# A windowed attention with a two-layer feed-forward: three of chunk 0's four head pairs in another arithmetic form, and three moves at the start

## The chip, the cores and the metric

The kernel runs on one core of a Trainium2 chip. The metric is the device time of one execution in microseconds. Before the change, three runs gave a median of 1069.58 us (1069.06 to 1069.76). One more execution was taken with the profiler; its own time is in the table below.

The names of the engines in the profile: PE is the matrix engine (TensorE) and PEld its weight load, DVE is VectorE, ACT is ScalarE, POOL is GpSimd, SP is the queue that issues most transfers. A name with a small q behind it (ACTq, SPq) is that engine's instruction queue, where transfers are issued.

## What is computed

```python
# q, k, v: 8 batches x 8 heads x 576 positions x 64
scores = scale * np.matmul(q, k.transpose(0, 1, 3, 2))
mask = (rel >= 0) & (rel < 128)              # a window of 128 positions
scores = np.where(mask, scores + bias, -1e9) # bias: slope of the head times distance
attn = softmax(scores)
x = (attn @ v), heads side by side           # 4608 tokens x 512
h = x @ w_in                                 # 512 x 2048
g = np.where(h >= 1, h, np.where(h <= -1, 0, (h + 1) ** 2 / 4))
out = g @ w_out                              # 2048 x 512
```

The weights w_in and w_out are given in double precision (64 bits), so the kernel has to convert them itself; everything else is float32.

## The kernel before, in words

The 4608 tokens are cut into 12 chunks of 384 (three blocks of 128). A chunk has eight heads, taken as four pairs, so there are 48 pairs `p` and 96 heads `m`: pairs 0 to 3 with heads 0 to 7 belong to chunk 0, pairs 4 to 7 to chunk 1, and so on. Each chunk then goes through the feed-forward in 16 steps `fc`, each with a slice of 128 of the 2048 hidden columns: `layer1` (12 products into one PSUM bank, L363 to L365), the activation (L372 on ScalarE, L373 and L374 on VectorE), and `layer2` (into three accumulator banks, L393 or L396 to L398).

One head goes through these steps:

- `scores` (L220): products of q and k into PSUM (L243 or L245, L246); VectorE adds the bias and mask and finds the row's extreme (L249, tile `z`); ScalarE takes the exponential and its sum (L251); VectorE takes the reciprocal of the sum (L257, L258) and folds the two halves of the window, scaled, into `ep` (L262, L264). There is one buffer `z`, so the next head's L249 can start only when this head's fold is done.
- `weights_t` (L267): three transposes on PE (L273), a copy out of PSUM on ScalarE (L276 or L283, tile `lu`), and two selects on GpSimd (L277 and L279, or L286 and L288) that cut the window's triangles.
- `values` (L292): products of these with v into `x`, then a copy into `xn`, which the feed-forward's `split_x` (L350) cuts into a high part `xh` (L356, ScalarE) and a low part `xl` (L357, VectorE).

There are two forms. In the **plain** form the products take float32 operands with 64 rows (q times k, L243) or 64 columns (L314). In the **split** form each operand is cut into a high part in the type fp32r and the rest; the two parts lie side by side in the 128 rows or columns of the array, and there are two products for each block (L245 and L246; L338). The split form costs more operations outside PE: `prepare_q` takes two ScalarE and two VectorE operations (L198, L199) for one ScalarE operation (L193); `prepare_k` (L208 ScalarE, L209 VectorE) and `prepare_v` (L217, L218) exist only there; `weights_t` has one more VectorE operation (L284) and selects twice as wide; `values` ends with one copy and two additions for each head (L339, L340, L342). In chunk 0 before, a pair's two heads write into the two halves of one bank, and one copy (L319) takes both out.

`LIGHT = 2` makes the first two chunks plain. The loads of k are into tag `kr`, and for odd pairs of the plain form into tag `kk`, which is otherwise the split form's high part; each tag has one buffer. The same holds for v with tags `vn` and `vs`.

The order of the work: `segments` is a list of all attention steps, head by head, up to head 13 in the order scores, preparation of the next pair, `weights_t` of the head before, `values` of the head before that. During chunk 0's attention the weights of the first feed-forward steps are fetched (L123 and L129, on ScalarE's queue) and converted (`convert_in` and `convert_out`, L113 to L116, L135 and L136), at the places that `EARLY` lists. After `values(7)` the feed-forward's steps follow, with the attention of the next chunk spread between them. The framework's scheduler then orders the instructions of each engine by readiness, with the program's order as priority; on the chip each engine runs them strictly in that order. `behind(ins, f)` adds an ordering on the engine of `ins`: what `f` issues on that engine comes after `ins`.

Of the kernel before, what the change touches and what calls it, by code (L numbers as in the profile page):

```python
# [8 lines left out]
F32 = mybir.dt.float32  # L9
# [9 lines left out]
def windowed_attention_then_ffn(  # L19
# [37 lines left out]
    assert 2 * SEQ == CYCLE * CH and CYCLE == 3 and CUT == P + D  # L57
    NEG = -1.0e30

    LIGHT = 2  # L60

# [16 lines left out]
    quarter = const.tile([P, 1], F32, name="quarter")  # L78
    G.memset(quarter, 0.25)
    qscale = const.tile([P, NPAIR], F32, name="qscale")  # L80
    for g in range(NPAIR):
# [71 lines left out]
    head = {}  # L153
    xn = {}
    done_t = {}
    lo_rows = [slice(0, D), slice(D, P)]
# [6 lines left out]
    def load_qk(p):  # L163

        c, g = divmod(p, NPAIR)
        n = CH + before(c) * P
        st = pair[p] = {}
        qr = st["qr"] = ap1.tile([P, CH], F32, name=f"qr_{p}", tag="qr")
        DMA.dma_start(qr, q[g * P:(g + 1) * P, c * CH:(c + 1) * CH])
        kr = st["kr"] = ap1.tile([P, 2, CH + P], F32, name=f"kr_{p}", tag="kk" if c < LIGHT and p % 2 else "kr")  # L170
        if c < LIGHT:
            DMA.dma_start(kr[:, 0, :n], k[g * P:(g + 1) * P, (c + 1) * CH - n:(c + 1) * CH])
            return
        for half in (slice(0, D), slice(D, P)):
            DMA.dma_start(kr[half, :, :n],
                          k[g * P:(g + 1) * P, (c + 1) * CH - n:(c + 1) * CH].rearrange("(j d) t -> d j t", j=2))

    def load_v(p):
        c, g = divmod(p, NPAIR)
        nb = NQB + before(c)  # L180
        if c < LIGHT and p % 2:
            t = ap1.tile([P, 2, NQB + 1, 2, D], F32, name=f"vn_{p}", tag="vs")[:, 0]
        else:
            t = ap1.tile([P, NQB + 1, 2, D], F32, name=f"vn_{p}", tag="vn")
        pair[p]["vn"] = t
        DMA.dma_start(t[:, :nb].rearrange("p i j d -> p i (j d)"),
                      v[(c + 1) * CH - nb * P:(c + 1) * CH, g * P:(g + 1) * P].rearrange("(i p) d -> p i d", p=P))

    def prepare_q(p):
        ql = pair[p]["ql"] = ap1.tile([P, 2, CH], F32R, name=f"ql_{p}", tag="ql")  # L190
        qr = pair[p]["qr"]
        if p // NPAIR < LIGHT:
            S.activation(ql[:, 0].bitcast(F32), qr, AF.Copy, scale=qscale[:, p % NPAIR:p % NPAIR + 1])  # L193
            return
        for j in range(2):
            scale = 2.0 ** (2 * (p % NPAIR) + j + 1) / 8.0
            o_hi, o_lo, s = ql[lo_rows[j], j], ql[hi_rows[j], j], qr[lo_rows[j]]
            S.mul(o_hi, s, scale)  # L198
            V.scalar_tensor_tensor(o_lo, s, scale, o_hi.bitcast(F32), ALU.mult, ALU.subtract)  # L199

    def prepare_k(p):
        if p // NPAIR < LIGHT:
            return
# [7 lines left out]
    def prepare_v(p):  # L211
        if p // NPAIR < LIGHT:
            return
# [6 lines left out]
    def scores(m, blks):  # L220
# [14 lines left out]
        for n, i in enumerate(blks):  # L235
# [4 lines left out]
            win.append((o, c0, lone))  # L240
            if c < LIGHT:
                r, qs, ks = lo_rows[j], slice(i * P, (i + 1) * P), slice(k0, k0 + 2 * P - c0)
                T.matmul(o, ql[r, 0, qs].bitcast(F32), kr[r, 0, ks], start=True, stop=True)  # L243
                continue
# [22 lines left out]
    def weights_t(m):  # L267
# [4 lines left out]
        for i in range(NQB):  # L272
            T.transpose(pt[:, i, :], ep[:, i, :], ident)  # L273
        if m < LIGHT * H:
            own = lu[:, 0, 1::2, :].bitcast(F32)
# [16 lines left out]
    def values(m):  # L292
# [4 lines left out]
        if j == 0:  # L297
            xn[c, g] = xp1.tile([P, CH], F32, name=f"xn_{c}_{g}", tag=f"xn{g}")
        if c == 0:

            if j == 0:
                pair[p]["px"] = ps_acc.tile([P, DM], F32, name=f"x_{m}", tag="acc")
            pb = pair[p]["px"]
        else:
            pb = bank(f"x_{m}")
        px, pf = pb[:, :CH], pb.rearrange("r (i w) -> r i w", w=P)
        o = xn[c, g][lo_rows[j]]
        if c < LIGHT:
            po = px[lo_rows[j]] if c == 0 else px[:D]
            todo = [i for i in (0, 1, 2, -1) if i + b0 >= 0]  # L310
            for n, i in enumerate(todo):
# [4 lines left out]
                         start=(n == 0), stop=(n == len(todo) - 1), skip_group_check=True)  # L316
            if c == 0:
                if j:
                    (V.tensor_copy if g % 2 else S.copy)(xn[c, g], px)  # L319
            elif j:  # L320
                S.copy(o, po)
# [8 lines left out]
        for n, (i, s) in enumerate(todo):  # L330
# [5 lines left out]
            else:  # L336
                ox, lx = px[:, q0 * P:q1 * P], lu[:, s, first:first + q1 - q0, :].rearrange("p a w -> p (a w)")
            T.matmul(ox, w, lx, start=(n == 0), stop=(n == len(todo) - 1), skip_group_check=True)  # L338
        S.copy(o, px[D:, :])  # L339
# [98 lines left out]
    for i in range(NCHUNK * NFC + LAG):  # L438
        c, fc = divmod(i, NFC)
        ops = []  # L440
        if c < NCHUNK:
            if fc == 0:
                ops.append(lambda c=c: split_x(c))
            ops.append(lambda c=c, fc=fc: layer1(c, fc))
            if c == 0:
# [28 lines left out]
    load_v(0)  # L474
    prepare_q(0)
    prepare_k(0)
    load_qk(1)
    for fc in range(2):
        fetch_weights(fc)
    for t, m in enumerate(EARLY):  # L480
# [45 lines left out]
```

## Time and profile before

| | |
|---|---|
| median of three runs | 1069.58 us |
| the profiled execution, its own time | 1071.97 us |
| its span (first to last instruction) | 1070.3 us |
| mean granted TensorE clock over the span | 0.99 |
| PE busy | 1034.4 us (97%) |
| VectorE busy | 790.2 us (74%) |
| ScalarE busy | 619.1 us (58%) |
| GpSimd busy | 370.6 us (35%) |

The page gives busy times of whole executions. Other views used below: the windows give the busy time of each engine in chosen stretches of the span, with the granted TensorE clock; the chain of waits follows the work that ended last back in time; the timeline lists instructions with their start and duration; the groups by line give the count, the total and the mean duration (ns) of one kind of instruction, behind the second bar its idle time in front; the issues of transfers give KB and the time from issue to landing. Within brackets a row of the timeline tells how long the engine stood idle before it and what released it.

### The profile page before, as it was taken

Reading aid. Unit: us, or ns where it says so; the run is one execution under the profiler, and the core shown is the slowest. Engines: PE = TensorE matmul, PEld = TensorE weight load, DVE = VectorE, ACT = ScalarE, POOL = GpSimd, SP = SyncE. Lnnn points to the kernel's source line nnn. Section 1 sums busy time; section 2 is a strip of 40 time slices with the busy share of each in tenths; the row PEclk is TensorE's granted clock in tenths of the full one; section 3 lists DMA queues with packets and bytes.
Section 4 is the critical chain, followed back from the end, with each engine's and each line's share of the span. In section 5 each row is a group of like instructions: output and inputs, shape, how many; then the busy total and the mean of one; then the engine's idle time right before and its main releaser. Section 6 shows DMA issues by size and latency. Waiting matters only on the chain.

```text
span 1070.3 us, 16779 instructions
## 1 busy us (share of the span) xinstructions
PE 1034.4 (97%) x5472; PEld 900.9 (84%) x5472; DVE 790.2 (74%) x2249; ACT 619.1 (58%) x1475; POOL 370.6 (35%) x419
## 2 busy tenths in 40 slices
PE   6899999999999999999999999999999999999998
PEld 3566667998988988998998989899899889899996
DVE  3687799888887688877678887767787897862322
ACT  4686876556655556556557556555565665742322
POOL 2121003334443343443343443443334444332221
PEclk9889999999999999999999999999999999999999
DMA  5455512121122122121211212111121221200000
GB/s 190 139 188 189 175 45 69 34 59 60 45 65 67 39 62 79 33 56 35 66 47 50 82 47 65 63 30 37 60 65 37 77 65 38 76 1 1 30 1 30
DMA packets 58903, 69.50 MB, mean 65 GB/s; under 512 B 4032, under 2 KB 44480, under 8 KB 58816
## 3 DMA queue, kind: packets, MB, share of 16 engines
q1 hardware_dynamic: 48064, 51.66, 16.8%
q10 hardware_dynamic: 10752, 16.78, 4.5%
q8 instruction: 43, 0.70, 0.3%
q14 instruction: 44, 0.36, 0.1%
HBM read 58.98 MB, written 9.44 MB: 64 GB/s over the span
## 4 chain that ended last, share of the span: by engine, by line
PE 82%; DVE 8%; ACT 5%; issue 2%; POOL 2%; DMA 0%; ACTq 0%; DVEq 0%; POOLq 0%
PE h L363 11%; PE h L364 11%; PE h L365 11%; PE acc L396 10%; PE acc L397 10%; PE acc L398 10%; PE x L338 5%; PE acc L393 3%; PE p L273 3%; PE s L246 2%; PE s L245 2%; PE x L314 2%; PE s L243 2%; ACT z L251 1%; POOL lu L288 1%
## 5 line engine op out<-in xcount | busy, mean ns | idle before, releaser
L382 POOL TENSOR_TENSOR gl<-g,gh 128x384 fp32r<-128x384 f32 x176 | 184.1, 1046 | 434.9 <-ACT gh L381 422.0
L363 PE MATMUL h<-xh,wi 128*128 128x384 f32 x768 | 265.0, 345 | 1.8 <-ACT sg L372 1.6
L364 PE MATMUL h<-xl,wi 128*128 128x384 f32 x768 | 260.3, 339 | 0.6 <-DVE xl L357 0.6
L365 PE MATMUL h<-xh,wi 128*128 128x384 f32 x768 | 259.4, 338 | 0.0
L396 PE MATMUL acc<-wo,gh 128*128 128x512 f32 x528 | 211.8, 401 | 8.1 <-ACT gh L381 8.1
L373 DVE SCALAR_TENSOR_TENSOR g<-sg 128x384 f32<-128x384 f32 x192 | 108.6, 565 | 150.4 <-ACT sg L372 139.0
L397 PE MATMUL acc<-wo,gh 128*128 128x512 f32 x528 | 207.8, 394 | 0.0
L381 ACT CAST gh<-g 128x384 fp32r<-128x384 f32 x176 | 90.4, 513 | 192.5 <-DVE g L374 182.1
L372 ACT ACTIVATE sg<-h,quarter 128x384 f32<-128x384 f32 x192 | 111.2, 579 | 141.4 <-PE h L365 140.6
L251 ACT ACTIVATE z<-z,nmax 128x256 f32<-128x256 f32 (+2 forms) x288 | 139.2, 486 | 33.8 <-DVE nmax L249 31.7
L398 PE MATMUL acc<-wo,gl 128*128 128x512 f32 x528 | 155.5, 398 | 0.0
L363 PEld LDWEIGHTS h<-xh,wi 128*128 128x128 f32 x768 | 144.5, 188 | 11.0 <-ACT sg L372 3.2
L364 PEld LDWEIGHTS h<-xl,wi 128*128 128x128 f32 x768 | 144.5, 188 | 7.2 <-issue 2.0
L365 PEld LDWEIGHTS h<-xh,wi 128*128 128x128 f32 x768 | 144.4, 188 | 0.0
L249 DVE CUSTOM_DVE_ANT_0 z<-s,rel 128x256 f32<-128x256 f32 (+2 forms) x256 | 94.3, 394 | 52.8 <-PE s L246 43.3
L264 DVE CUSTOM_DVE_ANT_0 ep<-z,rc 128x128 f32<-128x128 f32 x256 | 129.4, 546 | 1.5
L286 POOL TENSOR_SCALAR_AFFINE_SELECT lu<-lu 128x768 fp32r<-128x768 f32 x80 | 80.7, 1008 | 128.7 <-DVE lu L284 120.1
L396 PEld LDWEIGHTS acc<-wo,gh 128*128 128x128 f32 x528 | 99.4, 188 | 27.3 <-ACT gh L381 10.5
L374 DVE SCALAR_TENSOR_TENSOR g<-sg,g 128x384 f32<-128x384 f32 x192 | 111.9, 583 | 3.7
L398 PEld LDWEIGHTS acc<-wo,gl 128*128 128x128 f32 x528 | 97.0, 188 | 19.7 <-POOL gl L382 0.2
L397 PEld LDWEIGHTS acc<-wo,gh 128*128 128x128 f32 x528 | 99.4, 188 | 16.5
L288 POOL TENSOR_SCALAR_AFFINE_SELECT lu<-lu 128x768 fp32r<-128x768 f32 x80 | 81.3, 1017 | 4.6
(78 smaller groups left out, 1451.4 us busy)
## 6 DMA issues: line engine op xcount, KB each, us to landing
kr<-in_k_dram SPq DMA_DIRECT2D x60, 256.0 KB, 3.8
qr<-in_q_dram SPq DMA_DIRECT2D x48, 192.0 KB, 3.4
out_dram<-o SPq DMA_DIRECT2D x36, 256.0 KB, 2.3
rawi<-in_moe_w_in_dram ACTq DMA_DIRECT2D x16, 512.0 KB, 3.9
rawo<-in_moe_w_out_dram ACTq DMA_DIRECT2D x16, 512.0 KB, 5.0
vn<-in_v_dram SPq DMA_DIRECT2D x32, 256.0 KB, 2.7
kr<-in_k_dram SPq DMA_DIRECT2D x28, 192.0 KB, 3.2
vn<-in_v_dram SPq DMA_DIRECT2D x16, 192.0 KB, 2.5
```

The costliest lines, as they stand in the source:

```text
L251: S.activation(z[:, i, c0:], z[:, i, c0:], AF.Exp, bias=nmax[:, i:i + 1], scale=-1.0, accum_out=sm[:, i, 0:1])
L264: st["folded"] = V.tensor_tensor_reduce(out=ep[:, i, :], in0=z[:, i, :P], in1=z[:, i, P:], op0=ALU.add, op1=ALU.add, scale=rc[:, i:i + 1], ...
L363: T.matmul(ph, wi[fc][:, 0, cc, :], xh, start=(cc == 0), stop=False)
L364: T.matmul(ph, wi[fc][:, 0, cc, :], xl, start=False, stop=False)
L365: T.matmul(ph, wi[fc][:, 1, cc, :], xh, start=False, stop=(cc == NCC - 1))
L372: first = S.activation(sg, ph, AF.Relu, bias=quarter[:, 0:1], scale=0.25)
L373: V.scalar_tensor_tensor(g, sg, 0.5, sg, ALU.min, ALU.mult)
L374: last = V.scalar_tensor_tensor(g, sg, -0.25, g, ALU.add, ALU.max)
L382: G.tensor_tensor(gl, g, gh.bitcast(F32), ALU.subtract)
L396: T.matmul(a, gh[:, ts], wo[fc][:, 0], start=first, stop=False)
L397: T.matmul(a, gh[:, ts], wo[fc][:, 1], start=False, stop=False)
L398: T.matmul(a, gl[:, ts], wo[fc][:, 0], start=False, stop=last)
```

## The change

Four things:

1. The plain form is now used for pair 0 and for chunk 1 (pairs 4 to 7). Pairs 1 to 3, that is heads 2 to 7, take the split form. Pair 0's two heads no longer share a bank; each has a bank of its own and a copy of its own.
2. An exponential of a 128 x 1 tile is issued on ScalarE as soon as its constant is there.
3. The fetches of the first two weight slices are ordered behind the scaling of pair 0's q on ScalarE's queue.
4. The 12 products of `layer1(0, 0)` are ordered on PE behind the last product of the last split head's `values` (head 7).

```diff
-    LIGHT = 2
+    def plain(p):
+        return p == 0 or NPAIR <= p < 2 * NPAIR
...
     G.memset(quarter, 0.25)
+    loaded = const.tile([P, 1], F32, name="loaded")
+    S.activation(loaded, quarter, AF.Exp)
...
+    last_x = [None]
...
-        kr = st["kr"] = ap1.tile([P, 2, CH + P], F32, name=f"kr_{p}", tag="kk" if c < LIGHT and p % 2 else "kr")
-        if c < LIGHT:
+        kr = st["kr"] = ap1.tile([P, 2, CH + P], F32, name=f"kr_{p}", tag="kk" if plain(p) and p % 2 else "kr")
+        if plain(p):
...
-        if p // NPAIR < LIGHT:
-            S.activation(ql[:, 0].bitcast(F32), qr, AF.Copy, scale=qscale[:, p % NPAIR:p % NPAIR + 1])
-            return
+        if plain(p):
+            return S.activation(ql[:, 0].bitcast(F32), qr, AF.Copy, scale=qscale[:, p % NPAIR:p % NPAIR + 1])
...
-        if m < LIGHT * H:
+        if plain(m // 2):
...
-        if c == 0:
-
-            if j == 0:
-                pair[p]["px"] = ps_acc.tile([P, DM], F32, name=f"x_{m}", tag="acc")
-            pb = pair[p]["px"]
-        else:
-            pb = bank(f"x_{m}")
+        pb = ps_acc.tile([P, DM], F32, name=f"x_{m}", tag="acc") if c == 0 else bank(f"x_{m}")
...
-            po = px[lo_rows[j]] if c == 0 else px[:D]
+            po = px[:D]
...
-            if c == 0:
-                if j:
-                    (V.tensor_copy if g % 2 else S.copy)(xn[c, g], px)
-            elif j:
+            if j:
                 S.copy(o, po)
             else:
                 V.tensor_copy(o, po)
...
-            T.matmul(ox, w, lx, start=(n == 0), stop=(n == len(todo) - 1), skip_group_check=True)
+            last_x[0] = T.matmul(ox, w, lx, start=(n == 0), stop=(n == len(todo) - 1), skip_group_check=True).ins
...
-            ops.append(lambda c=c, fc=fc: layer1(c, fc))
+            if c == 0 and fc == 0:
+                ops.append(lambda: behind([last_x[0]], lambda: layer1(0, 0)))
+            else:
+                ops.append(lambda c=c, fc=fc: layer1(c, fc))
...
-    prepare_q(0)
+    scaled = prepare_q(0)
     prepare_k(0)
     load_qk(1)
-    for fc in range(2):
-        fetch_weights(fc)
+    behind([scaled.ins], lambda: [fetch_weights(fc) for fc in range(2)])
```

The other tests of `c < LIGHT` (in `load_v`, `prepare_k`, `prepare_v`, `scores`, `values`) become `plain(p)` in the same way.

More of the change, by code (lines that the diff above doesn't have):

```diff
@@ L180, in load_v @@
         nb = NQB + before(c)
-        if c < LIGHT and p % 2:
+        if plain(p) and p % 2:
             t = ap1.tile([P, 2, NQB + 1, 2, D], F32, name=f"vn_{p}", tag="vs")[:, 0]
@@ L201, in prepare_k @@
     def prepare_k(p):
-        if p // NPAIR < LIGHT:
+        if plain(p):
             return
@@ L211, in prepare_v @@
     def prepare_v(p):
-        if p // NPAIR < LIGHT:
+        if plain(p):
             return
@@ L240, in scores @@
             win.append((o, c0, lone))
-            if c < LIGHT:
+            if plain(p):
                 r, qs, ks = lo_rows[j], slice(i * P, (i + 1) * P), slice(k0, k0 + 2 * P - c0)
@@ L298, in values @@
             xn[c, g] = xp1.tile([P, CH], F32, name=f"xn_{c}_{g}", tag=f"xn{g}")
-        if c == 0:
-            if j == 0:
-                pair[p]["px"] = ps_acc.tile([P, DM], F32, name=f"x_{m}", tag="acc")
-            pb = pair[p]["px"]
-        else:
-            pb = bank(f"x_{m}")
+        pb = ps_acc.tile([P, DM], F32, name=f"x_{m}", tag="acc") if c == 0 else bank(f"x_{m}")
         px, pf = pb[:, :CH], pb.rearrange("r (i w) -> r i w", w=P)
         o = xn[c, g][lo_rows[j]]
-        if c < LIGHT:
-            po = px[lo_rows[j]] if c == 0 else px[:D]
+        if plain(p):
+            po = px[:D]
             todo = [i for i in (0, 1, 2, -1) if i + b0 >= 0]
```

## The prediction

> **What bounds the kernel now.** I read the busy totals first, then the busy time by stage (the windows), then the chain of waits, then single rows of the timeline and the groups by line.
>
> ```profile
> PE 1034.4 (97%) x5472; PEld 900.9 (84%) x5472; DVE 790.2 (74%) x2249; ACT 619.1 (58%) x1475; POOL 370.6 (35%) x419
> ```
> ```profile
> 17.84:51.00 33.16, 30.48 (x102) 16.84 (x101) 22.09 (x96) 22.34 (x63) 7.02 (x13) 0.85 0.48 155
> 27.00:36.00 9.00, 7.33 (x27) 3.91 (x25) 8.19 (x30) 8.14 (x23) 2.42 (x4) 0.78 0.55 174
> 36.00:43.00 7.00, 7.00 (x22) 4.18 (x20) 3.94 (x17) 2.14 (x7) 0.34 (x1) 0.55 0.54 194
> 58.45:67.30 8.85, 8.85 (x29) 5.92 (x28) 7.38 (x29) 5.75 (x15) 2.23 (x6) 0.56 0.49 156
> 67.00:75.00 8.00, 8.00 (x36) 5.40 (x35) 7.67 (x26) 8.00 (x19) 2.18 (x3) 1.00 0.67 218
> ```
>
> Columns of the windows: length, then busy time of PE, PEld, DVE, ACT and POOL, then the granted TensorE clock. PE is busy for 97% of the span, and from 67 us on it is full at clock 1.00. The change takes no instruction out of that part. So it is worth what it does to the moment at which PE becomes full, and to the work still open at that moment. Everything is decided in the first 67 us, where chunk 0's eight heads must all be finished before the feed-forward can take its last input.
>
> In that part PE looks full as well (30.48 of 33.16 us), but at a low clock: 0.55 between 36 and 43 us, with 7.00 of 7.00 us busy. The chain shows what that does.
>
> ```profile
> 0.80 3.50 DMA qr<-in_q_dram
> ...
> 34.05 2.33 PE x L314 x6
> ...
> 44.97 1.30 PE x L314 x6
> ...
> 55.70 2.14 PE x L314 x6
> 57.85 2.64 PE s L243 x6
> ...
> 81.92 1.38 PE s L243 x6
> ```
>
> The same six products of `values` (L314) take 1.30 us at 44.97 and 2.33 at 34.05. For several stretches the chain runs from PE to PE. DVE is second: 8.19 of 9.00 us between 27 and 36 us (0.91), and 7.67 of 8.00 after 67 us (0.96).
>
> **The change part by part.** First the start.
>
> ```profile
> 4.37 1.28 ACT L193 ACT_TABLE_LOAD   x1 [4.37 <-DMA qr<-in_q_dram]
> 4.44 0.39 ACTq L123 DMA_DIRECT2D rawi<-in_moe_w_in_dram  x1
> 4.85 0.53 ACTq L129 DMA_DIRECT2D rawo<-in_moe_w_out_dram  x1
> 5.67 0.61 ACT L193 ACTIVATE ql<-qr,qscale 128x384 f32<-128x384 f32 x1
> 8.41 0.40 ACT L251 ACTIVATE z<-z,nmax 128x128 f32<-128x128 f32 x1 [2.13 <-DVE nmax L249]
> ```
> ```profile
> 6.33 3.09 PE L243 MATMUL s<-kr,ql 64*128 64x128 f32 x12 [6.33 <-ACT ql L193]
> ```
> ```profile
> 1.25 0.42 SPq L172 DMA_DIRECT2D kr<-in_k_dram  x1
> ```
> ```profile
> kr<-in_k_dram SPq DMA_DIRECT2D x1, 192.0 KB, 4.9
> ```
> ```profile
> 22.29 0.69 ACT L113 ACTIVATE rawi<-rawi 128x512 f32<-128x512 f32 x1 [0.52 <-issue]
> ```
>
> The table load begins only when q has landed (4.37) and holds the scaling of q until 5.67. With the dummy Exp it lies in the 3.50 us of q's transfer and costs nothing there; the scaling then starts 1.30 us earlier. What is late next is k: issued 0.45 us behind q, at 1.25, it landed 4.9 later, at 6.15, hardly before the scaled q (6.28). If k stays so late, the start gains only about 0.1 us. But the first weights no longer transfer beside it; if q and k both land as fast as the fastest such transfer below (3.1 us), the gain is 1.9. I take 1.5, nearer the upper end, because the weights were the only other large transfers in that time.
>
> The four weight transfers now issue behind the scaled q: 2 x (0.39 + 0.53) = 1.84 us of ACT's queue. The next ACT instruction is the first Exp, which waited 2.13 us for VectorE after the scaling; that hides them by 0.3 us, and without that cover they would cost up to 1.84. Their data is first read at 22.29, some 15 us after the last issue.
>
> Pair 1 pays at once. Its k goes to the buffer of pair 0's k (tag `kr`), so its load waits until pair 0's scores are done (before, it had tag `kk`, which was free). SP's queue holds the loads behind it for that time, which nothing needs yet.
>
> ```profile
> DMA to landing us min/median/max: 3.1/4.7/6.2
> ```
> ```profile
> 17.84 0.29 DVE L249 CUSTOM_DVE_ANT_0 z<-s,rel 128x128 f32<-128x128 f32 x1 [2.97 <-PE s L243]
> ```
> ```profile
> 50.92 0.42 DVE L249 CUSTOM_DVE_ANT_0 z<-s,rel 128x256 f32<-128x256 f32 x1
> ...
> 51.27 0.42 DVE L249 CUSTOM_DVE_ANT_0 z<-s,rel_end 128x256 f32<-128x256 f32 x1
> ```
> ```profile
> L208 ACT CAST kk<-kr 128x768 fp32r<-128x768 f32 x12 | 10.0, 836 | 1.6 <-PE s L245 1.4
> ```
> ```profile
> L199 DVE SCALAR_TENSOR_TENSOR ql<-qr,ql 64x384 fp32r<-64x384 f32 x74 | 55.3, 748 | 2.3
> L284 DVE TENSOR_TENSOR lu<-p,lu 128x384 fp32r<-128x384 f32 x75 | 41.6, 555 | 4.6 <-ACT lu L283 3.3
> L340 DVE TENSOR_TENSOR xn<-x,xn 64x384 f32<-64x384 f32 x76 | 41.5, 547 | 4.1 <-ACT xn L339 2.9
> ...
> L342 DVE TENSOR_TENSOR xn<-x,xn 64x128 f32<-64x128 f32 x76 | 21.2, 279 | 1.7
> ...
> L209 DVE TENSOR_TENSOR kl<-kr,kk 128x768 fp32r<-128x768 f32 x12 | 13.6, 1135 | 0.1
> ...
> L218 DVE TENSOR_TENSOR vs<-vn,vs 128x384 fp32r<-128x384 f32 x12 | 6.9, 573 | 0.0
> ```
>
> The first of these is the landing of k in the first 30 us. Pair 0's scores ended at 6.33 + 3.09 = 9.42; 1.5 earlier is 7.9. A k that takes the median 4.7, then the cast (0.84), the subtraction (1.14) and some 0.7 for the scores: VectorE starts head 2's scores at 15.3 instead of 17.84, a gain of 2.5 (with landings of 3.1 and 6.2: 13.7 and 16.8).
>
> Now the stage from head 2's first score operation on VectorE to head 8's, 17.84 to 50.92 before. In its 33.16 us VectorE was busy 22.09. The split form adds: q for two pairs, 4 x 0.748 = 3.0; k for two pairs, 2 x 1.135 = 2.3; v for three, 3 x 0.573 = 1.7; the low half of the transposed weights for five heads, 5 x 0.555 = 2.8; two additions for five heads, 5 x (0.547 + 0.279) = 4.1. Pair 0's new copy and pair 1's lost one cancel. That is 13.9, so 36.0 us of VectorE work in a stage that lasted 33.16. At the best density seen (0.96, 67 to 75 us) it takes 37.6; at 0.91 it takes 39.5; without any gap 36.0. I take 37.6, because behind each head there is always some other head's work to fill in. Head 8 then starts at 15.3 + 37.6 = 52.9, against 50.92: **+2.0**.
>
> PE would be no reason for delay in this stage. A split head's `values` need far less:
>
> ```profile
> 287.37 0.59 PE x L338 x5
> ```
>
> 0.59 us at full clock against 1.30, so some 1.2 against 2.33 at the low one. This is the real gain of the split form here, and the sum says that VectorE does not let it through.
>
> Next, from head 8's start to the end of the first product of the feed-forward (`layer1(0,0)`).
>
> ```profile
> 61.84 0.52 PE L365 MATMUL h<-xh,wi 128*128 128x384 f32 x1
> ```
> ```profile
> L288 POOL TENSOR_SCALAR_AFFINE_SELECT lu<-lu 128x768 fp32r<-128x768 f32 x75 | 76.3, 1017 | 4.2
> ```
> ```profile
> L277 POOL TENSOR_SCALAR_AFFINE_SELECT lu<-lu 128x384 f32<-128x384 f32 x16 | 10.2, 636 | 72.1 <-ACT lu L276 72.1
> ```
> ```profile
> L339 ACT COPY xn<-x 64x384 f32<-64x384 f32 x76 | 36.2, 476 | 14.5 <-PE x L338 11.2 <-DVE xl L357 1.8
> ```
> ```profile
> L357 DVE TENSOR_TENSOR xl<-xn,xh 128x384 fp32r<-128x384 f32 x4 | 2.2, 554 | 0.0
> ```
>
> Before: 50.92 to 62.36, 11.4 us, of which 6.9 to the end of `values(7)` at 57.85. After: those 6.9, plus 0.56 for the low half, plus 2 x (1.017 - 0.636) = 0.8 for the two selects, less 2.14 - 1.2 = 0.9 for the products, makes 7.4. Then copy 0.48, additions 0.55 + 0.28, subtraction 0.55 and a cast taken as long as it, three products at about 0.18 to 0.35 each and hand-offs, some 3.2 in all. The other nine products of `layer1(0,0)`, which were spread between the heads before, now stand behind the last values on PE; they fill the 2.4 us in which PE waits for the last cast, and cost nothing there (up to 3 us at the low clock without that cover). Together 10.6: **-0.8**. Queued behind them on PE are head 10's scores, which were done before (57.85 to 60.49) and are now still open, 1.38 at full clock: **+1.4**.
>
> Last, the clock. Between 58.45 and 67.30 PE was busy throughout at 0.56, so 8.85 x 0.44 = 3.9 us were lost. Afterwards twelve full-array products come in one run, which may wake the clock sooner; the half-array ones (64 rows at L243, 64 columns at L314) did not for 11 us. I take a gain of **1.0**, between 2.9 and a loss of 1.8 (4 us more at 0.56). [...]
>
> Sum: +2.0 - 0.8 + 1.4 - 1.0 = **+1.6 us**. The profiled execution took 1071.97 us (its span of 1070.3 and 1.67 around it), which would become 1073.6; the median of the runs shown is 1069.58, 2.4 below it, so I forecast 1071.2.
>
> **The rivals.** *A, the forecast: VectorE becomes the bound of chunk 0.* Its own range: k's landing (-1.6 to +1.5), the density (-1.6 to +1.9) and the clock (-1.9 to +2.8) do not all go one way; I give it 1068 to 1075.
>
> *B, faster: PE's low-clock products were the real limit.* For it: in the stage before, PE was busy 92% and VectorE only 67%, and busy times of VectorE overlap (the operation of 0.42 us at 50.92 is followed by the next at 51.27, 0.35 later), so 36.0 us of records may fit into 36.0 x 0.9 = 32 us or a little more, say 33.7. With k a little earlier (14.8) head 8 starts at 48.5, -2.4; then -0.8 + 1.4, and the clock's best case, -2.9: -4.7, so 1064.9. Against it: no window that I read has VectorE above 0.96.
>
> *C, much slower: the wider selects on GpSimd stretch VectorE.*
>
> ```profile
> L264 DVE CUSTOM_DVE_ANT_0 ep<-z,rc 128x128 f32<-128x128 f32 x201 | 108.3, 579 | 1.2
> ```
> ```profile
> L264 DVE CUSTOM_DVE_ANT_0 ep<-z,rc 128x128 f32<-128x128 f32 x40 | 13.3, 373 | 0.2
> ```
>
> The fold of the weights (L264) takes 579 ns from 200 us on, where GpSimd works much, and 373 in the first 125. If chunk 0's take the later value, three per head for six heads: 18 x 0.206 = 3.7 us, at density 0.96 3.9, on top of A: +5.5, 1075.1. It decides once the selects lie beside the folds in most heads. [...]
>
> **How the numbers follow.** No change here means within 0.2%, 2.1 us, about what a measurement of this kernel can tell. A gets 0.56 (slower 0.29, same 0.24, faster 0.03), B 0.33 (faster 0.32, same 0.01), C 0.11, slower. Together faster 0.35, same 0.25, slower 0.40. The range 1064.0 to 1076.5 reaches to B's and C's centres and leaves out about 0.1 on each side; A's own stands above.
>
> **What would show it.** Right: the table load before 3 us; the first scaled q near 4.4; head 2's first score operation near 15; VectorE at 0.9 or more from there to head 8's, which starts after 51; `layer1(0,0)` in one run; PE's low-clock rows at half their length. Wrong: VectorE below 0.85 in that stage with head 8 before 50 (B), L264 near 0.58 us there (C), or the last product of the first layer's first block before 60 us. A difference that arises after 75 us would break the whole argument.

## The result and the profile after

The changed kernel took **1082.93 us** (median of 4 runs, 1082.46 to 1084.44), the kernel before 1069.67 beside it: a ratio of 1.012 (95% interval 1.0098 to 1.0143). The forecast was 1071.2, the range ended at 1076.5. The profiled execution took 1082.55 us with a span of 1080.8, 10.5 more than before. Two of the kernels below have one execution each in a slow state (2578.85 and 1264.66 us), which the times given leave out.

First the busy row of the page after, and then the windows of the first 90 us and the 60 behind them, of the kernel before and of the changed one (length, then busy time of PE, PEld, DVE, ACT, POOL, then the granted clock).

```profile
PE 1028.5 (95%) x5466; PEld 904.4 (84%) x5466; DVE 808.9 (75%) x2278; ACT 627.3 (58%) x1490; POOL 375.7 (35%) x419
```
```profile
0.00:90.00 90.00, 75.92 (x270) 46.82 (x270) 60.65 (x247) 60.53 (x159) 18.99 (x51) 0.89 0.54 175
90.00:150.00 60.00, 60.00 (x249) 41.17 (x250) 46.43 (x115) 42.26 (x84) 4.72 (x9) 1.00 0.43 139
```
```profile
0.00:90.00 90.00, 59.03 (x224) 42.84 (x225) 69.67 (x242) 60.71 (x153) 21.92 (x46) 0.77 0.55 167
90.00:150.00 60.00, 60.00 (x253) 40.51 (x252) 47.67 (x127) 45.31 (x94) 7.47 (x13) 1.00 0.47 152
```

From 90 to 150 us PE has no idle time in either kernel, and over the rest of the span it has about the same in both (21.3 us after, 21.8 before, by the table further down). So what PE loses in the first 90 us is not made up. It idles 31.0 us of them (90 less 59.03), against 14.1 before. VectorE works 9.0 us more.

The chain of waits of the first 75 us after (start, duration, what), cut to the rows that carry it:

```profile
0.80 2.56 DMA qr<-in_q_dram
...
8.01 6.27 DMA kr<-in_k_dram
14.36 0.84 ACT kk L213
...
16.87 6.91 DMA kr<-in_k_dram
23.88 0.84 ACT kk L213
24.74 0.97 DVE kl L214
25.71 0.59 ACT z L256 x2
...
40.96 1.56 DVE kl L214
...
47.96 1.41 PE x L335 x5
...
52.61 0.88 DVE ep L269
```

Up to 26 us the chain is two transfers of k, 13.2 us of them. From there on it runs over VectorE and ScalarE; before it ran from PE to PE. VectorE's first score operation of head 2, head 3 and head 8, in its timeline:

```profile
17.57 0.29 DVE L254 CUSTOM_DVE_ANT_0 z<-s,rel 128x128 f32<-128x128 f32 x1 [0.93 <-PE s L251]
...
29.77 0.28 DVE L254 CUSTOM_DVE_ANT_0 z<-s,rel 128x128 f32<-128x128 f32 x1
...
60.31 0.42 DVE L254 CUSTOM_DVE_ANT_0 z<-s,rel 128x256 f32<-128x256 f32 x1
```

Head 3 starts 12.20 us behind head 2; before it was 3.34 (17.84 to 21.18):

```profile
21.18 0.29 DVE L249 CUSTOM_DVE_ANT_0 z<-s,rel 128x128 f32<-128x128 f32 x1
```

ScalarE's timeline tells why:

```profile
23.88 0.83 ACT L213 CAST kk<-kr 128x768 fp32r<-128x768 f32 x1 [3.81 <-DMA kr<-in_k_dram]
24.61 1.06 ACT L203 ACTIVATE ql<-qr 64x384 fp32r<-64x384 f32 x2
25.70 0.51 ACT L256 ACTIVATE z<-z,nmax 128x256 f32<-128x256 f32 x1
```

The cast of pair 2's k waits 3.81 us for its transfer, and head 2's last exponential (25.70), whose scores VectorE had done by 18.56, stands behind it in ScalarE's order. Head 2 can't be folded without that exponential, and head 3 can't use the one buffer `z` before that. A head is held by the k of a later pair.

Now the stage from head 2 to head 8 in two windows, the one with that wait and the five heads behind it:

```profile
17.57:29.77 12.20, 4.89 (x19) 3.51 (x18) 6.80 (x22) 6.40 (x15) 0.74 (x2) 0.78 0.77 183
29.77:60.31 30.54, 17.64 (x63) 13.40 (x63) 27.68 (x96) 20.72 (x57) 10.13 (x11) 0.56 0.36 112
```

In the second VectorE is busy for 0.91 of the time, at 6.1 us per head, with PE busy for 0.58. These are two different limits in one stage: a transfer first, VectorE afterwards.

### The profile page after: what moved, and what is told of

It reads as the page before. It is cut to its first block, busy times and chain, and to the rows that moved or that the text cites. A ratio compares the mean times of both kernels' runs of the same rounds, so it can differ in the third digit from the quotient of the medians.

```text
span 1080.8 us, 16825 instructions
## 1 busy us (share of the span) xinstructions
PE 1028.5 (95%) x5466; PEld 904.4 (84%) x5466; DVE 808.9 (75%) x2278; ACT 627.3 (58%) x1490; POOL 375.7 (35%) x419
## 3 DMA queue, kind: packets, MB, share of 16 engines
q1 hardware_dynamic: 48496, 52.25, 17.4%
## 4 chain that ended last, share of the span: by engine, by line
PE 81%; DVE 8%; ACT 4%; issue 2%; POOL 2%; DMA 1%; ACTq 0%; SPq 0%; DVEq 0%; POOLq 0%
PE h L360 11%; PE h L361 11%; PE h L362 11%; PE acc L393 10%; PE acc L394 10%; PE acc L395 10%; PE x L335 5%; PE acc L390 3%; PE p L278 3%; PE s L250 2%; PE s L251 2%; PE s L248 1%; DMA kr<-in_k_dram 1%; PE x L314 1%; POOL lu L293 1%
## 5 line engine op out<-in xcount | busy, mean ns | idle before, releaser
L360 PEld LDWEIGHTS h<-xh,wi 128*128 128x128 f32 x768 | 144.7, 188 | 10.4 <-ACT sg L369 3.2
L291 POOL TENSOR_SCALAR_AFFINE_SELECT lu<-lu 128x768 fp32r<-128x768 f32 x86 | 86.7, 1008 | 160.4 <-DVE lu L289 147.6
L394 PEld LDWEIGHTS acc<-wo,gh 128*128 128x128 f32 x528 | 99.8, 189 | 16.4
L335 PEld LDWEIGHTS x<-lu,vs 128*128 128x128 f32 x542 | 77.6, 197 | 26.8 <-POOL lu L293 22.6
```

The source lines that it names most:

```text
L335: last_x[0] = T.matmul(ox, w, lx, start=(n == 0), stop=(n == len(todo) - 1), skip_group_check=True).ins
L360: T.matmul(ph, wi[fc][:, 0, cc, :], xh, start=(cc == 0), stop=False)
L394: T.matmul(a, gh[:, ts], wo[fc][:, 1], start=False, stop=False)
```

## The experiments

Three theories were on record at first. **K**: pair 2's k comes too late, and ScalarE's order hands the wait to head 2. **V**: VectorE's added work is the bound, as forecast. **M**: the moves at the start do the harm. Later came **C**: the half granted clock is what costs. Ratios are to the kernel before on the same chip, whose single times scatter from 1068 to 1079 us. A ratio on record is not the quotient of the two medians (for the split form without the moves that would be 1.0096 instead of 1.0074), so nothing is built here on differences of 0.2%.

### The late k

**k of pairs 1 to 3 in buffers of their own** (idle weight buffers), so that their loads wait for nobody:

```diff
-        kr = st["kr"] = ap1.tile([P, 2, CH + P], F32, name=f"kr_{p}", tag="kk" if plain(p) and p % 2 else "kr")
+        if 1 <= p < NPAIR:
+            kr = st["kr"] = wp.tile([P, 2, CH + P], F32, name=f"kr_{p}", tag=f"wi{NFC - 1 - p}")
+        else:
+            kr = st["kr"] = ap1.tile([P, 2, CH + P], F32, name=f"kr_{p}", tag="kk" if plain(p) and p % 2 else "kr")
```

> The changed kernel, but k of pairs 1, 2 and 3 goes to three buffers of its own (weight buffers that are empty at that time), so that no load of k waits for an earlier pair. Theory K (pair 2's k is loaded too late, and ScalarE stands in front of its cast: heads 2 to 3 take 12.2 us instead of 3.3): head 3 starts at 20 to 22 us instead of 29.8, and most of the 8.6 us come back, 1074 to 1077 us in all. Theory V (VectorE's added work is the bound, as predicted): what is won there is lost again before head 8, which starts no earlier than 57, and the time stays within 2 us of 1083. Theory M (the three moves at the start do the harm): no change, 1082 to 1084.

1075.36 us, ratio 1.004 (1.0019 to 1.0062). Of the changed kernel's 1.2%, 0.8% are gone, some 8.5 us (7.6 by the two medians). Head 2 starts at 15.91 and head 3 at 19.19, and head 8 starts at 52.70, where V had put it no earlier than 57: K holds. Pair 1's k has a buffer of its own here too, so this mends more than pair 2's k alone. Its windows from head 2 to head 8, and from there to the first slice's activation:

```profile
15.91:52.70 36.79, 23.07 (x85) 17.64 (x83) 33.38 (x114) 26.54 (x70) 10.64 (x13) 0.60 0.45 140
52.70:71.50 18.80, 17.54 (x61) 12.84 (x61) 16.03 (x66) 14.20 (x38) 5.02 (x10) 0.61 0.34 110
```

Without the wait the whole stage runs at VectorE's density of 0.907.

**Slice 2 of the weights later**, together with slice 3 (which stays where it was, so slice 2 alone moves), in the changed kernel:

```diff
-        if not second:
-            behind(done_t[m], lambda: fetch_weights(fc + 2))
+        if t in (2, 4, 6):
+            for f in ([2, 3] if t == 2 else [fc + 2]):
+                behind(done_t[m], lambda: fetch_weights(f))
```

> The changed kernel (1082.93 us) with one edit: slices 2 and 3 of the weights are fetched one step later than now, behind the transposes of the next even head, so that they no longer land beside pair 2's k (issued at 16.2, landed at 23.8). Theory K says that the late k holds head 3. If its landing time is owed to the weights beside it (6.9 us against 2.6 us at the start), it lands near 20 instead of 23.8, z of head 3 moves from 29.8 to 26 or 27, and the total falls to 1079 to 1081 us. If the k transfer itself (two halves that go to partitions by rows of 64) is that long, nothing moves, 1082 to 1084 us.

1077.07 us, ratio 1.006 (1.0039 to 1.0081); head 3 starts at 26.93. The same k, now with no weights beside it, first its second transfer in the chain, then ScalarE's timeline:

```profile
18.22 3.35 DMA kr<-in_k_dram
```
```profile
21.67 0.83 ACT L213 CAST kk<-kr 128x768 fp32r<-128x768 f32 x1 [0.44 <-DMA kr<-in_k_dram]
...
23.07 0.51 ACT L256 ACTIVATE z<-z,nmax 128x256 f32<-128x256 f32 x1
```

The transfer takes 3.35 us instead of 6.91 and ScalarE waits 0.44 us instead of 3.81, so a good part of the lateness comes from the weights beside the transfer. The gain does not come from pair 1's k, which still lands beside slices 0 and 1: head 2 starts at 18.93, even later than in the changed kernel. The gain was larger than expected.

**Both cures together:**

> The changed kernel with both cures for the late k: k of pairs 1 to 3 in buffers of their own (1075.36 us alone) and slices 2 and 3 of the weights one step later (1077.07 us alone). Theory K: both mend the same wait, so together they give little more than the better one, 1073 to 1075.5 us, and what is left above 1066.9 is no wait for k. If they mend different things (k's buffer, and q of pair 1, which landed 7.3 us after its issue in the first of the two): 1068 to 1071 us.

1077.24 us, ratio 1.0059 (1.0041 to 1.0078): no more than either alone, and above the expected range. They mend the same wait, and the rest is hardly a wait for k: from head 2 to head 8 (15.54 to 54.56) VectorE is busy for 0.91 of the time, as with k apart.

**The split form without the three moves** (no early table load, weights at once, no order for the first product):

> The changed kernel without the three moves: only the split form for pairs 1 to 3. Theories K and V: as slow as the full change or slower by up to the 2.2 us of the start, 1082 to 1086 us. Theory M: near the kernel before, 1069 to 1073.

1081.33 us, ratio 1.0074 (1.0051 to 1.0097). M as the cause of the whole loss is out: without the moves the kernel is still far slower than before. But it came out a little faster than the changed kernel, not as slow or slower as K and V expected, so in the split form the moves together do some harm (the two intervals do not overlap, the medians are 1.6 us apart). Heads 2 and 3 are 5.88 us apart here (19.22 and 25.10), and head 8 starts at 58.49.

**The changed kernel with the first weights at once again:**

```diff
-    behind([scaled.ins], lambda: [fetch_weights(fc) for fc in range(2)])
+    for fc in range(2):
+        fetch_weights(fc)
```

> The changed kernel (1082.93 us) with the first two weight slices fetched at once again, as before the change; table load, split form and the order of the first product stay. Theory K in its wider form (the weights behind q land beside pair 1's k, issued at 7.25 and landed 7.0 later, and later slices beside pair 2's): k of pair 1 lands within 4.5 us, z of head 2 comes at 16 or before instead of 17.6, the wait between heads 2 and 3 shrinks to 6 us as in the split form without the moves, and the total is 1077 to 1080 us. If the weights at the start do no harm: 1082 to 1085 us, later by the lost 1 to 2 us of the first head.

1078.94 us, ratio 1.0081 (1.0055 to 1.0108), against 1.012 with the weights behind q. Heads 2 and 3 are 5.95 us apart, as expected, not 12.20. Pair 1's k takes 3.3 us from issue to landing instead of 6.2 (medians of its two transfers). But head 0 and with it that load are 2.45 us later, and head 0's values stand on PE ahead of head 2's scores (15.06 to 17.46), so head 2 starts at 19.45 and not by 16. So the move costs the split kernel some 0.4% (the two intervals just overlap), though it brings head 0 forward. It makes slices 0 and 1 land beside pair 1's k (1.53 MB of weights moved between 6.9 and 14.4 us), and it comes with an order on ScalarE in which the cast of pair 2's k precedes head 2's last exponential; with the weights at once that exponential is done at 22.5, just ahead of the cast. How much falls to the transfer and how much to the order was not told apart.

What the split kernels have in common is that their time follows the start of head 8: 52.70 with k apart (1075.36 us), 55.34 with the weights at once (1078.94), 55.41 with slice 2 later (1077.07), 58.49 without the moves (1081.33), 60.31 in the changed kernel (1082.93). The wait between heads 2 and 3 is the largest single piece of that lateness, but not all of it: without the moves it is halved, and head 8 is only 1.8 us earlier.

### The moves in the plain kernel

**The table load and the weights behind q, chunk 0 all plain:**

> The kernel before with the early table load and the first weights behind q, nothing else. Theories K and V: the start's 2.2 us pass through the chain from PE to PE, 1067 to 1068.5 us; if the chain has slack behind the first heads, 1069 to 1070. Theory M: slower than before, 1073 or more.

1066.91 us, ratio **0.9952** (0.993 to 0.9974): faster than both kernels. So the two moves are no harm in themselves, as M had it; they gain where no split k waits beside them. Its windows from head 2 to head 8 and on to the first activation:

```profile
13.47:44.28 30.81, 28.47 (x105) 16.68 (x103) 22.74 (x95) 22.43 (x63) 6.89 (x13) 0.83 0.53 169
44.28:57.61 13.33, 10.33 (x47) 6.43 (x45) 11.35 (x47) 10.37 (x30) 4.04 (x9) 1.00 0.46 155
```

**The table load alone:**

> The kernel before with the early table load alone, the weights fetched at once as before. The two moves together gave 1066.91 us. From the start of the first scores: the table load alone frees 1.3 us of ScalarE, but k and q land later beside the weights; z of head 0 near 7 instead of 5.7 and 8.0, total 1067 to 1070 us. If the gain of the two moves is all in the weights: 1069 to 1071 us.

1073.03 us, ratio 1.0023 (1.0003 to 1.0044): no gain, if anything a small loss. PE's first scores tell why:

```profile
6.66 2.64 PE L244 MATMUL s<-kr,ql 64*128 64x128 f32 x11 [6.66 <-DMA kr<-in_k_dram]
```

They start at 6.66, later than before (6.33), and it is k that releases them, 5.42 us after its issue at 1.24: the transfer is late beside the weights (the loads of k issued in the first 8 us have a median of 6.1 us to landing, against 4.1 with the weights behind q). The gain needs the weights out of its way.

**The order of the first product, in both forms.** In the plain kernel with the two moves it was added; in the changed kernel it was taken out.

> The kernel before with the early table load and the weights behind q (1066.91 us), and the third of the moves too: the first product of the feed-forward behind the last value product, chunk 0 staying in plain form. If the third move is good whatever the form of chunk 0 (in the split kernel, taking it out cost 4 us), 1062 to 1065 us. If it only mends what the split form's late attention spoils (TensorE's queue held by products that wait while values are due), 1066 to 1069 us, no change to the run without it.

> The changed kernel without the order that puts the first product of the feed-forward behind the last values. Theories K and V: within 2 us of 1083, since the nine products fill a wait either way. Theory M, in the form that this order is what costs: 1077 to 1080.

Plain: 1069.67 us, ratio 0.9986 (0.9967 to 1.0004), against 0.9952 without it: if anything a loss. Split without it: 1087.22 us, ratio 1.0127 (1.0084 to 1.0169), against 1.012 with it; the intervals overlap wholly. Whether the order helps the split form stays open.

**Slice 2 later in the plain kernel, by the same edit:**

> The kernel before with the early table load and the weights behind q (1066.91 us), and slices 2 and 3 of the weights fetched one step later, the edit that gave the changed kernel 6 us back. Theory K says that this edit helps through the k of pair 2, which the plain form does not cast on ScalarE: no change here, 1066 to 1068 us. If the weights beside q, k and v cost the plain form time as well, or if by it the stretch of half clock from 23 to 34 us falls away: 1062 to 1065 us.

1068.04 us, ratio 0.9976 (0.9954 to 0.9998). No gain, as K says: in the plain form nothing casts that k.

### VectorE's work or the clock

**VectorE's work alone.** The plain kernel with the two moves gets the split form's VectorE operations for pairs 1 to 3, on an idle buffer `dm`; nobody uses their results. One of the added places:

```diff
             ga = S.copy(own, pt)
+            if 2 <= m < H:
+                V.tensor_tensor(dm[:, :CH].rearrange("r (i w) -> r i w", w=P), pt, dm[:, CH:].rearrange("r (i w) -> r i w", w=P), ALU.subtract)
```

> The kernel before with the early table load and the weights behind q (the run of these two alone gave 1066.91 us, z of head 2 at 13.47, z of head 8 at 44.28), and added to it, as work whose results nobody uses, the VectorE operations of the split form for pairs 1 to 3: low halves of q, k and v, the low half of the transposed weights, and two additions per value product. TensorE's, ScalarE's and GpSimd's work stays plain. The output is the reference's. Theory V (VectorE's added work alone is what the split form costs): from z of head 2 to z of head 8 the stage grows from 30.8 us to 36 to 38 us, VectorE is busy for over 0.9 of it, and the total is 1072 to 1076 us. Theory C (the split form costs time chiefly because it halves TensorE's work in the stage and so leaves the granted clock low afterwards): the clock stays near 0.83 in the stage and at full speed from 40 us on, the attention and the products behind it keep their pace, and the total stays at or below 1070 us.

1073.49 us, ratio 1.0027 (1.0011 to 1.0042), against 0.9952 without them: 0.75%, some 8.0 us. The split form with k apart lies 0.88% above the same kernel (1.004 against 0.9952), 9.4 us. So VectorE's added work by itself brings most of what the split form costs when k is no longer late. (The added operations read the PSUM banks and the buffers of q, k and v, as the split form's do, and so can hold these longer too; the two were not told apart.) But not where V put it: the stage grew only from 30.81 to 33.67, and the rest came behind it.

```profile
15.35:49.02 33.67, 29.84 (x89) 16.40 (x88) 29.86 (x115) 21.30 (x61) 6.69 (x11) 0.71 0.45 145
```
```profile
48.00:64.00 16.00, 16.00 (x41) 9.24 (x41) 10.80 (x45) 8.40 (x23) 4.04 (x9) 0.51 0.36 111
```

Between 48 and 64 us PE is busy throughout at a clock of 0.51. This looks like C, and led to the next runs.

**More work for PE in the split kernel** (k apart), first as four repeats of each first score product, then as three products of constants in front of each head's transposes:

```diff
+            if c == 0:
+                for _ in range(4):
+                    T.matmul(o, ql[:, j, i * P:(i + 1) * P], kk[:, j, k0:k0 + 2 * P - c0], start=True, stop=True)
             T.matmul(o, ql[:, j, i * P:(i + 1) * P], kk[:, j, k0:k0 + 2 * P - c0], start=True, stop=False)
```
```diff
+        if 2 <= m < H:
+            for _ in range(3):
+                T.matmul(pt[:, :2, :].rearrange("r i w -> r (i w)"), ident, rel, start=True, stop=True)
         for i in range(NQB):
             T.transpose(pt[:, i, :], ep[:, i, :], ident)
```

> The changed kernel with k of pairs 1 to 3 in buffers of their own (1075.36 us, clock 0.60 from z of head 2 to z of head 8, 18.3 us from there to the last product of the first slice), and each block's first score product of chunk 0's split heads repeated four times ahead of the one that counts, 96 more products of split form: work for TensorE alone; the output is the reference's. Theory V: TensorE has room, so nothing is gained where VectorE is the bound, 1075 us plus or minus 1.5, or slower by what the repeats put in the way. Theory C: the granted clock of the stage rises from 0.60 to over 0.8, the scores and values of chunk 1 that stand ahead of the first slice's products halve in duration, and the total falls to 1070 to 1073 us.

> The changed kernel with k of pairs 1 to 3 in buffers of their own (1075.36 us; TensorE busy 23.1 of the 36.8 us from z of head 2 to z of head 8, clock 0.60), with three full-precision products of two constants put ahead of the transposes of each of heads 2 to 7, where TensorE waits for VectorE's folds: 18 products, about 1 us per head at full clock, whose result is overwritten. The output is the reference's. Theory V: the fill hides in the wait and changes nothing, or costs what sticks out, 1075 to 1079 us. Theory C: the clock of the stage rises above 0.75, the stretch from z of head 8 to the last product of the first slice falls from 18.3 towards 12 us, and the total falls to 1069 to 1073 us.

1079.54 us, ratio 1.0082 (1.0057 to 1.0107), and 1077.7 us, ratio 1.0061 (1.0037 to 1.0086). Windows of the second:

```profile
15.11:53.40 38.29, 28.60 (x120) 21.88 (x118) 35.41 (x113) 26.51 (x70) 11.36 (x12) 0.83 0.45 139
53.40:69.73 16.33, 13.70 (x49) 9.14 (x49) 14.35 (x54) 13.08 (x36) 4.64 (x9) 0.71 0.41 128
```

The clock of the stage rose from 0.60 to 0.83, as C wanted, and the stage did not get shorter: 38.29 us against 36.79, with VectorE busy 0.92 of it. C fails for this stage.

The single runs say the same, since each comes with its mean granted clock. With k apart one run had 0.997 and took 1075.56 us; nine had 0.975 to 0.983 and took 1074.73 to 1078.29. The plain kernel with the two moves took 1065.41 to 1068.1 at 0.996 and 0.997. At the same clock the split form is thus some 8 us slower (one run against eight). VectorE's work alone: at 0.991 and 0.992 1071.58 to 1073.57 us, at 0.981 1074.2 to 1075.69. That is 2 to 3 us for a difference in clock that is worth 10 us of TensorE's time (1070 x 0.01), and at the higher clock it still stands some 6 us above the kernel without that work.

**A pause in PE's work**, to see whether it costs a stretch of half clock. The first attempt ordered three fills on GpSimd behind head 7's transposes and head 6's first value product behind the fills:

> The kernel before with the early table load and the weights behind q (1066.91 us; its granted clock is at half speed from 23.4 to 33.8 us and at full speed from there on), with one pause put in: after the transposes of head 7 three fills of an idle buffer run on GpSimd, and the first value product of head 6 waits for them, about 2 us in which TensorE gets nothing to do, near 41 to 44 us. The output is the reference's. Theory V (TensorE has room; only VectorE's added work costs time): 1067 to 1069 us, the pause at most, and the clock as without it. Theory C (a gap in TensorE's work at this stage is followed by 10 us or more of half clock, in which TensorE is the bound, so that each such stretch costs some 5 us): a stretch of half clock begins within some us of the pause, and the total is 1071 to 1075 us.

```profile
L277 POOL MEMSET dm<- x3: 738/738/750, 2.7 to 5.0; 128x768 f32 x3
```

There was no pause: the fills ran between 2.7 and 5.8 us, because this ordering holds on one engine only. The run (1067.27 us, ratio 0.9959, 0.9941 to 0.9977) is a repetition of the plain kernel with the two moves. The second attempt used a dependency on data, head 6's second select done four times more:

> The kernel before with the early table load and the weights behind q (1066.91 us), and a real pause: head 6's second select on GpSimd is done four times more over the same data (which changes nothing), some 2.4 us, and the value products of head 6 wait for the last of them, near 41 to 45 us. The output is the reference's. Theory V (what counts is the work that stands in the way, the clock only follows): 1067 to 1070 us, the pause at most. Theory C (a pause brings 10 us or more of half clock, worth 5 us by itself): 1072 to 1075 us and a stretch of half clock right behind the pause.

```profile
47.55 1.12 POOL L284 TENSOR_SCALAR_AFFINE_SELECT lu<-lu 128x384 f32<-128x384 f32 x2
```
```profile
48.81 2.18 PE L319 MATMUL x<-lu,vn 128*64 128x256 f32 x6
```

Head 6's values do wait for the last select (to 48.67), but PE did head 8's scores and head 7's transposes meanwhile. 1066.1 us, ratio 0.9955 (0.9936 to 0.9974): no cost. What a true pause costs through the clock was not measured.

### Where TensorE's time went

Over slices of 1 us of each profiled execution: idle is the length not busy, slow is busy time times what the granted clock lacks, work is the rest (us, summed over the span).

| kernel | idle | slow | work |
|---|---|---|---|
| before | 35.9 | 9.9 | 1024.6 |
| changed | 52.3 | 13.5 | 1015.0 |
| changed, k apart | 45.7 | 15.7 | 1012.7 |
| k apart, with the fill | 42.2 | 11.6 | 1022.3 |
| plain, two moves | 33.7 | 6.8 | 1022.9 |
| the same, with VectorE's work | 33.3 | 17.4 | 1022.7 |

The sum is not sharp: in the repetition of the plain kernel with the two moves (the first attempt at a pause) the work comes out as 1030.0 instead of 1022.9, with the same 5472 products. Over all profiled executions here the plain kernels lie between 1022.7 and 1030.9, the split ones without added products between 1012.3 and 1015.0.

The split form did take some work off TensorE, 9.6 us by this pair of executions. It got 16.4 us of idle time and 3.6 us of slow time in exchange: 10.4 us more, which is the span's difference (10.5) but for rounding. Idle and slow time may stand for each other, which no single run shows. Where the fill kept the clock up, it took 7.6 us off both, and its own work was 9.6. With VectorE's work alone the whole loss stands as slow time in the profiled execution; since runs of that kernel at a higher clock took nearly as long, it would have to stand as idle time there, but no such run was profiled and this is not shown.

## Why the prediction was wrong

**The sign and rival A's mechanism held, the size did not: 11.7 us are missing between 1071.2 and 1082.93.** With k in buffers of its own the kernel took 1075.36, so some 7.6 of them go with the late k. The other 4.2 arose although head 8 then started when the forecast had it, so they lie behind it. By the steps of the prediction:

- **Start (1.5 us forecast).** q landed and the scaling began at 3.46, head 0 started 2.2 us earlier (8.02 to 5.81). The reason given was right, and the gain lies even above its upper end of 1.9.
- **A step that failed: "The four weight transfers now issue behind the scaled q", with a cost of nothing.** Its cover was argued for ScalarE's issue slots alone. What the four transfers land beside was not asked. It is pair 1's k, in a form that loads it in two transfers of 192 KB instead of one. Issued at 7.25, it came at 14.3; the forecast took 4.7 us from the issue. Head 2 started at 17.57, not at 15.3. With the weights at once the split kernel took 1078.94, though not by way of an earlier head 2.
- **The main step that failed: pair 2's k was not in the sum at all.** The prediction noted that pair 1's load waits for the buffer and did not carry this on to pair 2, whose load waits until pair 1's k has been subtracted (issued at 16.21), lands beside slice 2 of the weights and is cast on ScalarE ahead of an exponential that is due. This made the 12.20 us between heads 2 and 3. Own buffers for pairs 1 to 3 gave back 7.6 us, slice 2 later 5.9 (by the medians; 8.5 and 6.4 by the ratios), both together no more. This is the greater part of the missing time; it overlaps with the step above, and the two do not add up. "SP's queue holds the loads behind it for that time, which nothing needs yet" was the sentence that let it pass.
- **VectorE in the stage (37.6 us forecast).** Added work 13.9 forecast, 12.5 measured (22.01 to 34.49 from head 2 to head 8; the additions of four heads fall into it, not of five); density 0.96 forecast, 0.91 measured. The errors cancel, which is luck: five heads took 30.54 us where the forecast's rate gives 31.3, and with k apart head 8 started at 52.70, forecast 52.9. The mechanism was right, and so, by that luck, was the size.
- **From head 8 to the end of the first product (10.6 us).** By the same measure the changed kernel took 11.8 (60.31 to 72.15), 0.4 more than before and not 0.8 less; the products did not come in one run either, nine from 67.00 and the last three behind three transposes and six scores of chunk 1:

```profile
71.81 0.34 PE L362 MATMUL h<-xh,wi 128*128 128x384 f32 x1
```

  With k apart it took 18.3 (52.70 to 71.03): PE was busy 17.54 us of the window to the activation behind it at a clock of 0.61, and chunk 1's scores and values stood ahead. There this step failed, and with it the small gain of the clock: -1.0 was forecast, TensorE's slow time rose by 3.6. The +1.4 for scores queued behind was not measured by itself.
- **Rival B** (1064.9) had the split form's saving on PE right and VectorE's overlap wrong. **Rival C**, the wider selects, is there but small: the fold took 450 ns in the stage against 372, and the rows of `kl` and `vs` grew likewise:

```profile
L269 DVE CUSTOM_DVE_ANT_0 ep<-z,rc 128x128 f32<-128x128 f32 x12 | 5.0, 450 | 0.0
...
L214 DVE TENSOR_TENSOR kl<-kr,kk 128x768 fp32r<-128x768 f32 x2 | 2.6, 1302 | 4.4 <-ACT kk L213 4.4
...
L223 DVE TENSOR_TENSOR vs<-vn,vs 128x384 fp32r<-128x384 f32 x3 | 2.3, 774 | 0.0
```

  Twelve folds at 0.078 more, two `kl` at 0.167 and three `vs` at 0.201 make 1.9 us. Two of the folds (0.96 and 1.00 us) took some three times as long as the others, each beside one of the wide selects of GpSimd, as C has it; the other ten (0.34 or 0.35 us) had no select beside them. The rest was not traced to the selects:

```profile
52.53 0.96 DVE L269 CUSTOM_DVE_ANT_0 ep<-z,rc 128x128 f32<-128x128 f32 x1
```
```profile
52.48 0.86 POOL L291 TENSOR_SCALAR_AFFINE_SELECT lu<-lu 128x768 fp32r<-128x768 f32 x1 [5.07 <-DVE lu L289]
```

- **The low clock.** The prediction read off its row that the clock can stay low while PE is busy throughout, and a second row shows it: 16.00 of 16.00 us at 0.51 (48 to 64 us, VectorE's work alone). That twelve full-array products in one run may bring the full clock back sooner was the author's estimate, and no run shows it: in the changed kernel nine of them began at 67.00 and the clock was back between 68 and 69 us; in the kernel before, where they were spread between the heads, between 66 and 67. The 11 us that the prediction gives for the half clock were nearer 10, from 32 to 42 us (0.51) and again from 56 to 66 (0.50), by slices of 1 us.

What stays open: what sets the length of the stretches of half clock, and why the gain of the two moves in the plain kernel (4 us by the medians, 5 by the ratio) is larger than the 2.3 us at head 0. In the profiled executions the rest shows as less slow time (9.9 to 6.8).

## What to carry to other kernels

When a transfer is moved out of one transfer's way, look up whose way it is moved into: behind q the weights freed head 0 and, in the split form, landed beside the next pair's k, which took 6.2 us instead of 3.3. When a step gets a new operation that waits for a transfer on an engine that runs in order, list what stands behind it there; here a cast for pair 2, which waited 3.81 us for its transfer, held the exponential of pair 1. And saving work on the bound engine was worth nothing here while the next one could not feed it: some 10 us less of TensorE's work came with 16 us more of its idle time.

## What the runs showed of the hardware

Of the transfers of 192 KB, q took 2.56 us from issue to landing at the start of the changed kernel, with only q, k and v under way; pair 2's k took 6.91 from its second issue beside 1.00 MB of weights, and 3.35 without them (slice 2 later). The granted clock was at 0.50 for stretches of some 3 us (from 49 to 52, second attempt at a pause) to 48 us (from 26 to 74, split form without the moves) in the first 77 us, in different places in every kernel, also with TensorE busy throughout (16.00 of 16.00 us at 0.51, VectorE's work alone); from 90 to 150 us it was at 1.00 in the kernel before and in the changed one. A higher clock was worth little where VectorE set the pace: with the fill, 0.83 instead of 0.60, the stage from head 2 to head 8 took 38.29 us instead of 36.79. In the kernel before, a set of 29 runs went from 1077.58 us at a mean clock of 0.982 to 1068.75 at 0.992.
